# Induced attention and a leaky feed-forward net in one kernel: a first batch with later weights, unread products, maxima by column tiles, and half of the weight conversion on GpSimd

## The chip, the cores and the metric

The kernel runs on one core of a Trainium2 chip (trn2). The metric is the device time of one execution in microseconds; several executions give a median. The profile is one further execution, read by the hardware profiler. Engines are called as the profile calls them: PE is TensorE, PEld its weight loads, DVE is VectorE, ACT is ScalarE, POOL is GpSimd, SP is SyncE, which here issues nearly all transfers.

## The reference, cut to what matters

```python
def mab(q, kv):
    s = scale * (q @ kv.transpose(0, 2, 1))
    s = s - s.max(-1, keepdims=True)
    a = np.exp(s)
    a /= a.sum(-1, keepdims=True) + 1e-09
    return a @ kv
h = mab(I, x)                     # x: 4 batches of 12480 rows of 128; I: 32 inducing rows
x = mab(x, h).reshape(49920, 128)
h = x @ w_in                      # 128 -> 2048
g = np.maximum(0.01 * h, h)
return (g @ w_out).astype(np.float32)
```

The weights `w_in` and `w_out` reach the chip as 64-bit floats: pairs of 32-bit words that the kernel must turn into 32-bit floats itself.

## The kernel before, in words

**Tiling.** A batch of 12480 rows is six groups of 2048 rows (g0 to g5, each four tiles of 512 tokens) and a rest of 192 rows (`RG`). There are 98 tiles in all; after the first two ("quick") tiles, every tile runs through 16 blocks f of the hidden width. A tile's first products (`ffn_first`, 32 rows of the array each, four in parallel) give a PSUM bank, ACT takes the rectified high part (`high`, L1140), DVE the low part (`low`, L1144), and `ffn_second` or `products` multiplies both by `w_hi` and `w_lo` (three products). A rectified block can also be finished on POOL instead of DVE: ACT writes `g`, POOL makes a cast (`ghi`, L1114 or L1445) and a subtraction (`glo`, L1116 or L1447). This is called a far pair below.

**The first batch** (`first_batch`, L692) is written out by hand. SP issues 25 loads of x (`xr`, four per group) with a load of a weight chunk (`raw`, 512 KB) after the loads whose index is in `LOADS`. Then seven rounds follow, one per group in the order RG, g0, ..., g5. A round transposes its group on PE (`turn`, L725, 16 transposes) and copies it with ACT (L731), spreads the running maximum of the group before (`spread`, L478, called in `running`), multiplies the weighted rows of the group two before (L578) and computes its own scores (`columns_product`, L398). After the last round `DRAIN` lists what goes between the last steps, up to `normalise`, which gives h. In `ROUNDS` and `DRAIN` a string of letters stands for each place in that order: l steps the weight conversion, t and d turn a chunk of `w_in`, k issues an unread product.

**Weight conversion** (`from_double`, L198). Eight chunks (four of `w_in`, four of `w_out`), each of 128x512 values: a scaled copy on ACT (L211), then on DVE a mask (L216), a shift and or (L220), another mask (L226) and a product (L230), then one sum on POOL (L235). For `w_out` a chunk is then split: ACT casts `w_hi` (L286) and POOL subtracts to get `w_lo` (L288). These two are emitted by `parts_of_w_out` once the chunk's conversion has been emitted.

**The two quick tiles.** `quick` (L1023) computes the second attention of tiles 0 and 1 in a short way; its exponential `qy` (L1044) is an ACT instruction that the first `ffn_first` depends on through `A`. The two tiles are then multiplied alternately, four blocks at a time (`rounds`), with full-array second products (L1202). Blocks f = 4c to 4c+3 need chunk c of `w_hi` and `w_lo`. Between the blocks `others(u)` steps the rest of the conversion (`late`) and other lanes; u counts the blocks of both tiles.

**The rest** (`turn_over`, from tile 2 on) is ordered by a planner that runs while the kernel is built: it keeps a clock per engine, chooses the next instruction by the earliest start, and gathers those PE instructions that use the array in another tiling into clusters, since each switch of tiling costs time. `PATIENCE`, `IDLE`, `HURRY`, `AHEAD`, `PACE` are its waiting times in ns, and `WAITS` (38 numbers in us) delays the clusters one by one.

Engines execute their own instructions in the order in which they stand: an instruction that waits holds all behind it on that engine.

## Time and profile before

| what | us |
|---|---|
| median of 3 runs | 1435.7 |
| lowest and highest | 1434.36, 1436.16 |
| the profiled execution | 1436.48 |
| span of its instructions | 1434.7 |

| engine | busy us | share of the span |
|---|---|---|
| PE | 1418.0 | 99% |
| PEld | 1301.2 | 91% |
| POOL | 1178.9 | 82% |
| DVE | 1070.6 | 75% |
| ACT | 1066.0 | 74% |

A busy share counts an instruction from its start to its end, and PE's products overlap, so 99% does not say that no time is lost there. The chain of work that ended last, followed back from the last instruction, is PE for 94% of the span. A line such as L1171 can be a helper that many callers use.

### The profile page before, as it was taken

How to read it: one execution, taken by the hardware profiler on the slowest of the kernel's cores; microseconds unless marked ns; L12 is line 12 of the kernel's file. 1: busy time of each engine (PE TensorE's matmuls, PEld its weight loads, DVE VectorE, ACT ScalarE, POOL GpSimd, SP SyncE). 2: the span in 40 equal slices, each digit the busy share in tenths (PEclk: the TensorE clock that was granted, in tenths of full speed). 3: DMA queues.
4: the chain of work that ended last, by engine and by line, in shares of the span. 5: the costliest groups of instructions: out<-in, count | busy, mean ns of one | idle time of the engine just before them, and what ended most of it. 6: DMA issues, size and time to landing. Idle time of an engine off the chain costs nothing.

```text
span 1434.7 us, 60214 instructions
## 1 busy us (share of the span) xinstructions
PE 1418.0 (99%) x25207; PEld 1301.2 (91%) x25207; DVE 1070.6 (75%) x1913; ACT 1066.0 (74%) x1956; POOL 1178.9 (82%) x1237
## 2 busy tenths in 40 slices
PE   8999999999999999999999999999999999999998
PEld 6679899998889899998899999999989999999997
DVE  6777787776777787877777777877787876777664
ACT  6567777777777777777777787777777877778775
POOL 2369999899999888899999998885557588969996
PEclk9999999999999999999999999999999999999999
DMA  8055556433454553464445445534222333233231
GB/s 297 13 115 101 107 109 123 97 82 86 97 99 89 116 94 56 75 146 107 99 91 95 88 84 111 114 87 110 57 61 59 64 63 66 45 64 69 56 67 23
DMA packets 400703, 128.49 MB, mean 90 GB/s; under 512 B 373136, under 2 KB 375600, under 8 KB 400432
## 3 DMA queue, kind: packets, MB, share of 16 engines
q1 hardware_dynamic: 399328, 124.50, 41.7%
q8 instruction: 198, 3.24, 1.0%
q14 instruction: 73, 0.60, 0.1%
q10 hardware_dynamic: 1104, 0.15, 0.1%
HBM read 48.94 MB, written 25.56 MB: 52 GB/s over the span
## 4 chain that ended last, share of the span: by engine, by line
PE 94%; DVE 2%; ACT 1%; DMA 1%; issue 1%; POOL 1%; SPq 1%; DVEq 0%; ACTq 0%; POOLq 0%
PE bank L1171 87%; PE bank L398 3%; PE bank L578 2%; PE bank L1202 1%; DVE glo L1144 1%; PE bank L725 1%; DMA xr<-in_x_dram 1%; ACT ghi L1140 0%; DMA out_dram<-osb 0%; PE bank L820 0%; SPq L1012 0%; ACT xT L731 0%; POOL glo L1447 0%; PE bank L1058 0%; SPq L703 0%
## 5 line engine op out<-in xcount | busy, mean ns | idle before, releaser
L1171 PE MATMUL bank<-glo,w_hi 32*128 32x512 f32 (+1 forms) x6080 | 1165.1, 375 | 0.0
L1171 PE MATMUL bank<-ghi,w_hi 32*128 32x512 f32 (+1 forms) x6080 | 1164.7, 375 | 0.2
L1171 PE MATMUL bank<-ghi,w_lo 32*128 32x512 f32 (+1 forms) x6080 | 1164.8, 374 | 0.0
L1171 PE MATMUL bank<-A,hwhi 32*128 32x512 f32 (+1 forms) x3394 | 993.6, 373 | 0.8 <-DVE glo L1144 0.4
L1144 DVE SCALAR_TENSOR_TENSOR glo<-bank,ghi 128x512 fp32r<-128x512 f32 (+1 forms) x1047 | 687.2, 681 | 254.1 <-ACT ghi L1140 241.4
L1171 PEld LDWEIGHTS bank<-ghi,w_hi 32*128 32x128 f32 x6080 | 805.1, 184 | 16.5 <-issue 2.7
L1171 PEld LDWEIGHTS bank<-ghi,w_lo 32*128 32x128 f32 x6080 | 807.0, 184 | 12.4 <-issue 2.0
L1171 PEld LDWEIGHTS bank<-glo,w_hi 32*128 32x128 f32 x6080 | 806.8, 184 | 11.8 <-issue 1.0
L1140 ACT ACTIVATE ghi<-bank 128x512 fp32r<-128x512 f32 (+1 forms) x1047 | 608.0, 597 | 151.3 <-PE bank L1171 128.4
L1447 POOL TENSOR_TENSOR glo<-g,ghi 128x512 fp32r<-128x512 f32 (+1 forms) x513 | 656.0, 1279 | 41.1
L1171 PE MATMUL bank<-A,hwlo 32*128 32x512 f32 (+1 forms) x1697 | 586.2, 370 | 0.0
L1171 PEld LDWEIGHTS bank<-A,hwhi 32*128 32x128 f32 x3394 | 564.9, 184 | 16.6 <-DVE glo L1144 2.4
L1140 ACT ACTIVATE g<-bank 128x512 f32<-128x512 f32 (+1 forms) x521 | 311.2, 598 | 146.7 <-PE bank L1171 87.5
L1445 POOL CAST ghi<-g 128x512 fp32r<-128x512 f32 (+1 forms) x513 | 312.9, 610 | 106.5 <-ACT g L1140 80.0
L1171 PEld LDWEIGHTS bank<-A,hwlo 32*128 32x128 f32 x1697 | 299.9, 184 | 2.6 <-issue 0.2
L1481 DVE TENSOR_TENSOR part<-bank,part 128x512 f32<-128x512 f32 (+1 forms) x190 | 130.0, 685 | 60.7 <-PE bank L1171 38.3
L1492 POOL TENSOR_TENSOR part<-part 128x512 f32<-128x512 f32 (+1 forms) x95 | 121.4, 1277 | 22.5 <-DVE part L1481 22.1
L1474 ACT COPY part<-bank 128x512 f32<-128x512 f32 (+1 forms) x190 | 110.7, 584 | 12.4 <-PE bank L1171 10.5
L1229 DVE STREAM_TRANSPOSE osb<-part 128x512 f32<-128x512 f32 (+1 forms) x95 | 66.6, 701 | 6.6 <-POOL part L1492 4.9
L534 DVE STREAM_TRANSPOSE xT<-xc 128x512 f32<-128x512 f32 x72 | 46.5, 684 | 0.0
L455 ACT ACTIVATE e<-e,nm 128x512 f32<-128x512 f32 (+1 forms) x28 | 18.7, 667 | 22.9 <-DVE least L443 22.7
L936 POOL TENSOR_TENSOR y<-y,mx 128x512 f32<-128x512 f32 (+1 forms) x24 | 24.4, 1018 | 9.6 <-DVE mx L932 8.3
(135 smaller groups left out, 646.1 us busy)
## 6 DMA issues: line engine op xcount, KB each, us to landing
A<-both SPq DMA_DIRECT2D x376, 128.0 KB, 2.4
xr<-in_x_dram SPq DMA_DIRECT2D x96, 256.0 KB, 4.3
out_dram<-osb SPq DMA_DIRECT2D x382, 64.0 KB, 2.2
xc<-in_x_dram SPq DMA_DIRECT2D x288, 64.0 KB, 2.9
raw<-in_moe_w_in_dram SPq DMA_DIRECT2D x4, 512.0 KB, 6.6
raw<-in_moe_w_out_dram SPq DMA_DIRECT2D x4, 512.0 KB, 7.4
A<-both SPq DMA_DIRECT2D x48, 16.0 KB, 1.8
out_dram<-osb SPq DMA_DIRECT2D x48, 8.0 KB, 1.8
```

Source lines behind the costliest of these rows:

```text
L398: nc.tensor.matmul(dst, lhsT, rhs, start=True, stop=True)
L534: nc.vector.transpose(t[:, j, :], blk.rearrange("p n c -> p (n c)"))
L578: nc.tensor.matmul(hp[32 * k : 32 * k + 32, :C], ay[:rows_, 4 * q + k, :], xb[:rows_, k, :], start=(q == 0), stop=(4 * q + 4 >= K), tile_p ...
L1140: nc.scalar.activation(ghi, ph, AF.Relu)
L1144: nc.vector.scalar_tensor_tensor(out=glo, in0=ph, scalar=0.0, in1=ghi, op0=ALU.max, op1=ALU.subtract,)
L1171: nc.tensor.matmul(dst, w[32 * r : 32 * r + 32], woven(x[32 * r : 32 * r + 32]), start=start, stop=stop, tile_position=(32 * r, 0),)
L1229: nc.vector.transpose(osb[:, :n], total[:, :n])
L1445: nc.gpsimd.tensor_copy(ghi[:, :n], g[:, :n])
L1447: nc.gpsimd.tensor_tensor(out=glo[:, :n], in0=g[:, :n], in1=ghi[:, :n].bitcast(F32), op=ALU.subtract)
L1474: nc.scalar.copy(put, got)
L1481: nc.vector.tensor_tensor(out=put, in0=got, in1=put, op=ALU.add)
L1492: nc.gpsimd.tensor_tensor(out=total[:, :n], in0=total[:, :n], in1=part[:, :n], op=ALU.add)
```

## The change

1. `LOADS` moves every weight chunk's load four x loads (one group) later; the first chunk of `w_out` comes after the last x load.
2. `fill` issues products of the identity with itself that nobody reads: four in `setup`, and one at each f in `ROUNDS` and `DRAIN`.
3. `spread` always uses four column tiles with `e32`; before, the first batch used one full-array product.
4. `from_double`: the product that was one DVE instruction is two on POOL, so POOL now does a scaling of the low words (`tensor_scalar`), a product and the sum.
5. The steps of the conversion stand at other places: none in round g1 and before, steps in three rounds instead of four, other places in `DRAIN`, two more in the list after it, and in `others` one at every u below 8.
6. The planner's numbers change; `WAITS` has 37 entries.

```diff
-    LOADS = [4, 8, 12, 16, 20]
+    LOADS = [8, 12, 16, 20, 24]
...
     ROUNDS = [
-        ["", ""],
-        ["", "", "", "", "", "ll", ""],
-        *[["l", "l", "", "", "lll", "", "", ""]] * 4,
+        ["f", ""],
+        ["", "", "", "", "", "ff", ""],
+        [""] * 8,
+        *[["l", "l", "", "", "lll", "", "", ""]] * 3,
         ["l", "l", "", "", "l", "", "tt", ""],
     ]
-    DRAIN = ["", "", "ll", "lldkk", "", ""]
+    DRAIN = ["ll", "", "l", "lldkk", "llf", "f"]
...
-    EARLY, PREFER, YIELDING, PATIENCE = 250.0, 0.0, 200.0, 6000.0
-    IDLE, HURRY, APART, TAIL, WAITING, SOON = 1300.0, 1000.0, 60000.0, 5000.0, 3500.0, 3000.0
+    EARLY, PREFER, YIELDING, PATIENCE = 250.0, 0.0, 200.0, 8000.0
+    IDLE, HURRY, APART, TAIL, WAITING, SOON = 1100.0, 5500.0, 60000.0, 5000.0, 3500.0, 3000.0
...
     WAITS = [
-        12.8, 12.2, 0.1, 3.6, 1.0, 0.0, 6.6, 0.7, 0.0, 4.7, 0.0, 0.8, 8.8, 0.0,
-        1.1, 4.2, 7.6, 6.1, 10.9, 0.0, 4.0, 0.0, 3.2, 0.0, 9.8, 0.0, 5.7, 6.3,
-        8.3, 0.0, 9.5, 6.4, 7.7, 8.6, 2.7, 0.2, 9.2, 6.4,
+        12.8, 12.2, 0.1, 3.6, 0.0, 1.5, 6.6, 0.0, 0.8, 4.2, 0.0, 0.8, 2.5, 0.0,
+        1.1, 1.7, 7.6, 6.1, 10.9, 0.0, 4.0, 0.0, 3.2, 0.0, 9.8, 0.0, 5.7, 6.3,
+        12.1, 0.0, 9.1, 6.4, 7.7, 8.6, 2.8, 0.0, 4.7,
     ]
-    AHEAD = 100.0
-    PACE, STOCK = 41250.0, 4
+    AHEAD = 150.0
+    PACE, STOCK = 36000.0, 4
...
-        nc.vector.scalar_tensor_tensor(
-            out=tail, in0=low.bitcast(U32), scalar=2.0**-52, in1=b.bitcast(F32),
-            op0=ALU.mult, op1=ALU.mult,
-        )
-        spent(POOL, 1270.0, spent(DVE, 690.0))
+        nc.gpsimd.tensor_scalar(
+            out=tail, in0=low.bitcast(U32), scalar1=2.0**-52, scalar2=None, op0=ALU.mult
+        )
+        nc.gpsimd.tensor_tensor(out=tail, in0=tail, in1=b.bitcast(F32), op=ALU.mult)
         nc.gpsimd.tensor_tensor(out=dst, in0=a.bitcast(F32), in1=tail, op=ALU.add)
+        spent(POOL, 3400.0, clock[DVE])
...
+    FILLERS = 4
+
+    def fill():
+        while True:
+            pt = gen_ps("fill_ps")
+            nc.tensor.matmul(pt[:, :P], ident, ident, start=True, stop=True)
+            done(pt)
+            yield
...
+        for _ in range(FILLERS):
+            next(filling)
         pt = aux_ps("ind_ps")
...
-        if not quads[0]:
-            same = e128.rearrange("p j m -> p (j m)")
-            nc.tensor.matmul(dst, same, src, start=True, stop=True)
-            return on_array("f", 64.0, at, taken[0])
         for k in range(4):
...
-            one, weights, two, one, weights, one, weights, one, keep, one, two, late, one, two,
+            one, late, weights, two, one, weights, one, weights, one, late, keep, one, two, late, one, two,
...
-            if u % 2 == 0:
+            if u % 2 == 0 or u < 8:
                 step(late)
```

What the letters do to the order of the instructions is seen at three places. In the changed kernel's rows the lines are 10 to 14 higher (L300 is what L286 was, L1054 what L1044 was).

DVE at the end of the first batch, before (L597 adds up h, L324 copies a turned chunk, L1036 begins the quick tile):

```order
L597 SCALAR_TENSOR_TENSOR hacc<-hacc,al,bank_69 128x128
L656 TENSOR_SCALAR rz<-bank_71 128x1
L657 RECIPROCAL rz<-rz 128x1
L216 TENSOR_SCALAR cv_b<-raw 128x512
L597 SCALAR_TENSOR_TENSOR hacc<-hacc,al,bank_64 128x128
L220 SCALAR_TENSOR_TENSOR cv_a<-cv_a,cv_b 128x512
L226 TENSOR_SCALAR cv_b<-cv_a 128x512
L324 COPY winT<-bank_65 128x512
L1036 TENSOR_REDUCE qmx<-bank_71 128x4
```

The same place after the change:

```order
L607 SCALAR_TENSOR_TENSOR hacc<-hacc,al,bank_69 128x128
L666 TENSOR_SCALAR rz<-bank_71 128x1
L667 RECIPROCAL rz<-rz 128x1
L607 SCALAR_TENSOR_TENSOR hacc<-hacc,al,bank_65 128x128
L217 TENSOR_SCALAR cv_b<-raw 128x512
L221 SCALAR_TENSOR_TENSOR cv_a<-cv_a,cv_b 128x512
L338 COPY winT<-bank_66 128x512
L227 TENSOR_SCALAR cv_b<-cv_a 128x512
L1046 TENSOR_REDUCE qmx<-bank_71 128x4
```

Before, the chunk converted here is the second of `w_out` (the sixth of all); after, it is the first of `w_out` (the fifth), with its second mask behind the copy of the turned chunk.

ACT at the same time, before (`hs` and `hT` end the first batch, L1044 is the quick tile's exponential):

```order
L211 ACTIVATE cv_a<-raw 128x512
L674 ACTIVATE hs<-hacc,rz 128x128
L684 COPY hT<-bank_70 128x128
L286 CAST w_hi<-wraw 128x512
L1044 ACTIVATE qy<-qy 128x128
L805 ACTIVATE hwhi<-bank_70 128x512
L1064 CAST A_685<-bank_67 128x512
```

And after:

```order
L212 ACTIVATE cv_a<-raw 128x512
L684 ACTIVATE hs<-hacc,rz 128x128
L694 COPY hT<-bank_70 128x128
L300 CAST w_hi<-wraw 128x512
L212 ACTIVATE cv_a<-raw 128x512
L1054 ACTIVATE qy<-qy 128x128
L815 ACTIVATE hwhi<-bank_70 128x512
L1074 CAST A_721<-bank_67 128x512
```

The cast of the first chunk of `w_hi` stands ahead of the exponential in both; a further chunk's scaled copy has come between them.

POOL from the first `w_lo` on, before:

```order
L288 TENSOR_TENSOR w_lo<-wraw,w_hi 128x512
L235 TENSOR_TENSOR wraw<-cv_a,cv_t 128x512
L288 TENSOR_TENSOR w_lo<-wraw,w_hi 128x512
L1114 CAST ghi<-g 128x512
L1116 TENSOR_TENSOR glo<-g,ghi 128x512
L1114 CAST ghi<-g 128x512
L1116 TENSOR_TENSOR glo<-g,ghi 128x512
```

And after:

```order
L302 TENSOR_TENSOR w_lo<-wraw,w_hi 128x512
L1124 CAST ghi<-g 128x512
L1126 TENSOR_TENSOR glo<-g,ghi 128x512
L1124 CAST ghi<-g 128x512
L1126 TENSOR_TENSOR glo<-g,ghi 128x512
L231 TENSOR_SCALAR cv_t<-raw 128x512
L234 TENSOR_TENSOR cv_t<-cv_t,cv_b 128x512
L235 TENSOR_TENSOR wraw<-cv_a,cv_t 128x512
L302 TENSOR_TENSOR w_lo<-wraw,w_hi 128x512
```

The second chunk of `w_out` stood ahead of the first two far pairs and now stands behind them.

## Rows read from the trace of the kernel before

**Rows 1.** Stretches: length, busy time and count by engine, granted clock, DMA share, GB/s.

```profile
91.34:1417.00 1325.66, 1324.20 (x24391) 1234.29 (x24390) 997.21 (x1731) 1008.09 (x1838) 1140.53 (x1198) 1.00 0.43 87
...
11.86:15.27 3.41, 3.41 (x18) 3.41 (x18) 0.53 (x2) 1.75 (x3) 0.00 (x0) 0.50 1.02 396
15.27:31.30 16.03, 15.84 (x206) 11.46 (x205) 15.42 (x52) 14.30 (x32) 5.63 (x4) 1.00 1.04 367
```

**Rows 2.** Chain that ended last, first 50 us in order: start, length, what.

```profile
11.74 3.62 PE bank L725 x16
...
25.28 1.90 PE bank L725 x16
...
29.36 0.60 PE bank L725 x4
...
39.87 0.23 PE bank L680 x2
...
42.21 0.32 ACT qy L1044
...
45.42 0.70 PE bank L1171 x8
```

**Rows 3.** The last x load of the first batch: its issue and its time to landing.

```profile
L703 SPq DMA_DIRECT2D xr<-in_x_dram x1: 328/328/328, 23.5 to 23.5; - x1
...
DMA to landing us min/median/max: 6.4/6.4/6.4
```

**Rows 4.** DVE in order of time, end of the first batch: start, length, instruction.

```profile
38.49 0.35 DVE L597 SCALAR_TENSOR_TENSOR hacc<-hacc,al,bank 128x128 f32<-128x128 f32 x1 [0.34 <-PE bank L578]
38.75 0.69 DVE L220 SCALAR_TENSOR_TENSOR cv_a<-cv_a,cv_b 128x512 int32<-128x512 int32 x1
...
39.81 0.68 DVE L324 COPY winT<-bank 128x512 f32<-128x512 f32 x1
```

**Rows 5.** ACT in order of time, the same place.

```profile
36.84 0.68 ACT L211 ACTIVATE cv_a<-raw 128x512 f32<-128x512 f32 x1
...
40.29 0.62 ACT L286 CAST w_hi<-wraw 128x512 fp32r<-128x512 f32 x1
```

**Rows 6.** POOL in order of time, quick tiles.

```profile
50.78 1.27 POOL L288 TENSOR_TENSOR w_lo<-wraw,w_hi 128x512 fp32r<-128x512 f32 x1 [4.08 <-ACT w_hi L286]
...
56.47 0.61 POOL L1114 CAST ghi<-g 128x512 fp32r<-128x512 f32 x1 [1.45 <-ACT g L1140]
57.16 1.29 POOL L1116 TENSOR_TENSOR glo<-g,ghi 128x512 fp32r<-128x512 f32 x1
```

**Rows 7.** PE in order of time, quick tiles.

```profile
60.24 0.48 PE L1202 MATMUL bank<-ghi,w_hi 128*128 128x512 f32 x1
...
71.74 0.48 PE L1202 MATMUL bank<-ghi,w_lo 128*128 128x512 f32 x1 [0.32 <-POOL w_lo L288]
...
74.31 1.64 PE L1171 MATMUL bank<-A,hwhi 32*128 32x512 f32 x4
...
82.65 0.48 PE L1202 MATMUL bank<-ghi,w_lo 128*128 128x512 f32 x1 [0.64 <-POOL w_lo L288]
```

**Rows 8.** Stretches of row-tiled products alone (L1171): length, PE and PEld busy.

```profile
277.48:317.27 39.79, 39.79 (x731) 37.72 (x731) 1.00 0.34 78
...
592.66:636.66 44.00, 43.59 (x792) 41.74 (x792) 1.00 0.46 94
...
1282.56:1417.02 134.46, 134.40 (x2446) 130.45 (x2446) 1.00 0.29 58
```

**Rows 9.** DVE masks, and a small scaling: durations in ns, min/median/max.

```profile
L216 DVE TENSOR_SCALAR cv_b<-raw x8: 381/428/1294, 9.8 to 69.2; 128x512 int32<-128x512 int32 x8
...
L953 DVE TENSOR_SCALAR sm<-sm x28: 124/547/1054, 65.1 to 1315.1; 128x16 f32<-128x16 f32 x24, 96x2 f32<-96x2 f32 x4
```

**Rows 10.** DVE and POOL in order of time, 68.9 to 70.6 us.

```profile
68.93 1.27 POOL L1116 TENSOR_TENSOR glo<-g,ghi 128x512 fp32r<-128x512 f32 x1
...
69.25 1.29 DVE L216 TENSOR_SCALAR cv_b<-raw 128x512 int32<-128x512 int32 x1
```

3 lines of the change are left out of this document (2 added, 1 removed).

## The prediction

> **What bounds the kernel now.** I read the stretches first, then the chain of waits in order of time, then each engine's instructions in order around the places that the change touches. From 91.3 us to 1417 us PE is busy for 1324.2 of 1325.7 us [rows 1]: the change can touch this part only through the pace of the products. The first 91 us are another matter. The chain there runs from a transfer to 11.74 us, when PE begins the transposes of the second full group; from then on it is PE, round after round, one round being 29.36 - 25.28 = 4.08 us [rows 2]. After the last transposes it is a chain of short dependent steps, through the quick tile's exponential at 42.21 us to the first feed-forward product at 45.42 us [rows 2]. In the two quick tiles PE is nearly closed up, but here and there it waits for a chunk of `w_lo` from POOL [rows 7]. So the question is what the change does to the chain of the first 91 us.
>
> My sum is made against the profiled execution, 1436.48 us, which is 0.8 us above the median of 1435.7; at the end I take the 0.8 off. A difference of 0.2%, 2.9 us here, is about what a measurement of this kernel can tell from none.
>
> **The change part by part.**
>
> *Later weights, unread products, column tiles (the first batch).* They work on one stretch, so they go together. What they can bring has a floor. The last x load was issued at 23.5 us and landed 6.4 us later, at 29.9 us [rows 3]. The transfers were full from 15 to 31 us, at 367 GB/s [rows 1]. One weight chunk of 0.52 MB now comes behind the last x load, which is worth 0.52 / 367 GB/s = 1.4 us: the load lands at 28.5. A quarter of its group's 16 transposes takes 1.90 / 4 = 0.5 us [rows 2], so the transposes cannot end before 29.0; before they ended at 29.36 + 1.90 = 31.26. **The gain is 2.3 us at most.** That the second group's transposes took 3.62 us at a granted clock of 0.50 (1.2 GHz) [rows 1, 2] instead of 1.90 at 2.4 GHz is part of the same 2.3 us and not to be added. The cheaper spread saves part of its time in each round, inside the same floor. The other end is nothing, if the rounds stay 4.08 us long for another reason (see the lock below). I take -1.2, the middle.
>
> *The unread products near the end.* One stands ahead of the product that makes hT, which is on the chain. The nearest row, a product of the same size, took 0.23 us [rows 2]: +0.2, between 0 and 0.3. The ones at the start lie in time in which PE has no data.
>
> *The cast of `w_hi` ahead of the exponential.* This is a new wait, and the largest doubt about the change. ACT has, in this order, the first cast of `w_hi`, now also a scaled copy of 0.68 us [rows 5], and then the exponential. Before, the chunk to be cast had been ready for long: the cast ran at 40.29 with no wait in front of it [rows 5]. Now this chunk is a conversion later, and its last DVE mask stands behind a mask, a shift-or and the copy of a turned chunk. I count from the last sum of h, which ended at 38.49 + 0.35 = 38.84 [rows 4]. Then DVE does a mask (0.43, the median in [rows 9]), a shift-or (0.69), the copy of a turned chunk (0.68) [rows 4] and a mask (0.43): 41.07. POOL does a product and a sum, for which its two-input row stands, 1.29 each [rows 6]: 43.65. Its scaling of the low words needs only the raw load and runs ahead. ACT casts (0.62) and copies (0.68) [rows 5]: the exponential can start at 44.95 instead of 42.21. All later work hangs on it: **+2.7**. If successive DVE instructions overlap a little, as the starts at 38.75 and 39.81 allow, it is 2.3; with one blocked instruction more it is 4.0.
>
> *PE's clock in that wait.* PE has only odd products while it waits. Before, a wait for x at the start was followed by 3.4 us at 1.2 GHz [rows 1]. If that comes again it can cost half of 3.4, 1.7 us; else nothing. Since part of that stretch is waiting anyway, I take +0.4.
>
> *The second chunk of `w_out`.* Behind two far pairs on POOL it becomes late. The second pair ended at 57.16 + 1.29 = 58.45 [rows 6]. Then POOL does the scaling: no row shows it; a cast of the same shape took 0.61 and a two-input operation 1.29 [rows 6], and as it reads one tensor I take 0.7. Product and sum make 2.58: 61.73. The cast on ACT, 0.62: 62.35. PE wants this chunk of `w_hi` at 60.24 [rows 7], so it stands for 2.1 us. POOL's subtraction takes 1.27 [rows 6]: `w_lo` is there at 63.62, while PE could use it 0.3 us after `w_hi`: another 1.0 us. **+3.1**; 2.7 with every price at its low end, 4.4 with one instruction blocked. Meanwhile ACT holds the next rectified blocks back behind the cast, but PE is late by more than they are.
>
> *What this repays.* PE waited 0.32 and 0.64 us for the third and fourth chunks of `w_lo`, and four first products at 74.31 took 1.64 us, where the usual four take about 0.5 [rows 7]. With PE 3 us later, and the third chunk no longer behind a far pair, most of it goes: -1.5, between 0 and -2.1.
>
> *Less conversion on DVE, the planner's numbers.* In the rest, the order shows 46 low parts fewer on DVE and 46 far pairs more on POOL, and one entry less in `WAITS`. A pair is 0.61 + 1.29 = 1.9 us [rows 6], 87 us in all; POOL had 1326 - 1141 = 185 us free [rows 1]. What PE gains depends on the pace. A clean stretch runs at 39.79 / 731 = 54.4 ns a product, two slow ones at 55.6 and 55.0 [rows 8]; at the clean pace these two would give 0.9 and 1.3 us. I set the low end at twice their sum, -4.5, since other stretches are slow too, and the high end at +2, for new waits for POOL. No row says which, so I take 0.
>
> **The sum:** -1.2 + 0.2 + 2.7 + 0.4 + 3.1 - 1.5 + 0 = +3.7 us, 1440.2 for an execution like the profiled one, 1439.4 for the median.
>
> **The lock.** A DVE mask began at 69.25 while POOL's subtraction ran until 70.20, and took 1.29 us instead of 0.43; eight such masks go up to 1294 ns, and a small scaling from SBUF to SBUF, 28 times, has a median of 547 and goes from 124 to 1054 [rows 9, 10]. So some DVE instructions wait until POOL's instruction is over. The change makes POOL busy for 0.7 + 2.58 = 3.3 us per chunk in rounds of 4.08 us, while DVE still does two masks and a shift-or for the next chunk. The Trainium skill (SBUF — State Buffer, Who interferes with whom) says that DVE and GpSimd share a port pair as an exclusive lock: a DVE instruction in a two-port mode, or with two SBUF inputs against a GpSimd instruction that reads SBUF, blocks for the other's whole instruction. By that rule the 1.29 us of this trace is the full wait and would meet all three conversion steps, the case of the first rival, 1444.2, against 1439.4 without it; the trace agrees for the masks.
>
> **The rivals.**
>
> *Blocked conversions (slower still).* The mechanism is the row at 69.25. In each of three rounds DVE would wait out the rest of a POOL instruction and another, 0.65 + 0.65 us, of which about half fits into DVE's spare time of a round: the gain of the first batch turns into about +1, and the two waits go to 4.0 and 4.4. The sum is then 1 + 0.2 + 4.0 + 0.4 + 4.4 - 1.5 = +8.5, 1444.2. For it speaks that the spread of durations is real; against it that half of the places lie where DVE waits for PE anyway.
>
> *The floor is reached and the waits are short (no change).* The first batch gives its 2.3, the clock stays up, both new waits cost their low ends and the old ones go: -2.3 + 0.2 + 2.3 + 2.7 - 2.1 = +0.8, 1436.5. For it: PE set the pace of the rounds, and its waits go with the new order of the loads.
>
> *The pace of the long part (not slower).* Moving 46 low parts off DVE closes the slow stretches. It decides from a mean of about 54.4 ns a product in the stretches that now take 55 and more. With the full 4.5 us the sum is -0.8, 1434.9; together with the case before it is -3.7, 1432.0, and faster. Against it: in [rows 8] PE is busy throughout, and POOL would be at 93%.
>
> *The unread products do not hold the clock.* Then the second group's transposes again run at 1.2 GHz and the first batch gives nothing: +4.9, 1440.6.
>
> **How the numbers follow.** The forecast has 0.45, with a range of its own from 1437.5 to 1442; blocked conversions 0.09, the floor 0.23, the pace of the long part 0.17, the clock 0.06. The predicted time is the forecast's, 1439.4. Slower by over 0.2% means above 1438.6: four fifths of the forecast, the blocked conversions and the clock, 0.51. Within 0.2%: the rest of the forecast, most of the floor and part of the pace, 0.36. Faster: the pace with the floor, 0.13. The range from 1432.5 to 1442.5 leaves out the blocked conversions and the best of the combined case.
>
> **What would show it.** Right: the first feed-forward product comes later than 45.4 us, with ACT idle in front of the cast of `w_hi` until a POOL sum; PE waits some 2 us for the second chunk's `w_hi`, released by ACT, and then for `w_lo`; the row-tiled part begins near 95 us instead of 91.3; DVE masks of over 0.6 us among the conversions. Wrong: no such idle time on ACT, a first product before 44 us, or a long part shorter than 1322 us.

## The result, and the profile after

The changed kernel takes 1452.85 us (median of 6 runs, 1448.51 to 1454.95) against 1435.74 us (6 runs, 1434.09 to 1436.16): a ratio of 1.0115, 95% interval 1.0105 to 1.0126. The forecast was 1439.4 with a range up to 1442.5. The sign was right; of some 17 us it had 3.7. The six executions of the changed kernel do not agree well: two lie at 1448.5 to 1448.7 us and four at 1452.8 to 1455.0.

The profiled execution took 1448.73 us with a span of 1446.9. Three places cut the time of either profile into four stretches: the last score products of the first batch (the line L398, after the change L412), the first second-product of the quick tiles (L1202, L1212), and the first row-tiled product behind the last of those. They can be read off each profile's PE in order of time; the last stretch ends with PE's last product.

| stretch, us | before | after | difference |
|---|---|---|---|
| start to the last score products | 32.09 | 31.18 | -0.91 |
| from there to the first second-product | 15.23 | 18.31 | +3.08 |
| from there to the row-tiled part (quick tiles) | 44.02 | 55.38 | +11.36 |
| row-tiled part | 1338.42 | 1337.14 | -1.28 |
| sum | 1429.76 | 1442.01 | +12.25 |

So 12.25 us of the 17 can be found in these two profiles, and nearly all of them lie in the quick tiles. The profiled execution is one of the two short ones; the other 4 to 5 us of the median lie outside it (see "Two executions of one kernel"). Stretches of the changed kernel, in the columns of [rows 1]:

```profile
65.84:71.30 5.46, 4.89 (x15) 3.94 (x16) 4.71 (x7) 3.72 (x8) 5.18 (x4) 0.50 0.10 14
71.30:83.66 12.36, 12.36 (x86) 8.28 (x85) 11.99 (x22) 5.76 (x11) 6.28 (x7) 1.00 0.28 44
83.66:87.82 4.16, 0.16 (x1) 0.00 (x0) 0.13 (x1) 0.02 (x1) 3.95 (x3) 1.00 0.18 28
87.82:95.40 7.58, 6.50 (x23) 4.67 (x27) 3.59 (x7) 2.84 (x6) 2.28 (x2) 0.55 0.67 124
104.87:1429.27 1324.40, 1324.23 (x24392) 1234.24 (x24391) 971.01 (x1684) 1003.74 (x1838) 1222.45 (x1292) 1.00 0.43 87
```

From 83.66 to 87.82 every engine but POOL stands still. Behind the two long waits PE works at a mean granted clock of 0.50 and 0.55 (the lower of its two levels, 1.2 GHz, for all or most of the stretch). The last line is what [rows 1] had as 1325.66 us.

PE of the changed kernel in order of time, the waits that are new against [rows 2, 7]:

```profile
31.18 1.07 PE L412 MATMUL bank<-xT,indT 128*32 128x512 f32 x8 [1.14 <-ACT xT L741]
...
40.02 0.49 PE L246 MATMUL bank<-ident 128*128 128x128 f32 x2 [1.39 <-DVE winT L338]
40.34 0.39 PE L690 MATMUL bank<-e,hs 128*128 128x128 f32 x2
...
49.49 0.48 PE L1212 MATMUL bank<-ghi,w_hi 128*128 128x512 f32 x1 [0.68 <-ACT ghi L1150]
...
65.84 0.79 PE L1212 MATMUL bank<-ghi,w_hi 128*128 128x512 f32 x1 [3.35 <-ACT w_hi L300]
67.20 0.79 PE L1212 MATMUL bank<-ghi,w_lo 128*128 128x512 f32 x1 [0.56 <-POOL w_lo L302]
...
87.82 1.50 PE L363 MATMUL bank<-wraw,winT 128*128 128x128 f32 x8 [4.00 <-POOL wraw L235]
...
91.69 0.80 PE L839 MATMUL bank<-w,hT 128*128 128x128 f32 x2 [1.08 <-DVE w L369]
```

POOL at the two long waits, where [rows 6] showed the far pairs with the conversion already done:

```profile
55.23 0.61 POOL L1124 CAST ghi<-g 128x512 fp32r<-128x512 f32 x1 [10.18 <-ACT g L1150]
...
59.33 1.29 POOL L1126 TENSOR_TENSOR glo<-g,ghi 128x512 fp32r<-128x512 f32 x1
60.71 1.75 POOL L231 TENSOR_SCALAR cv_t<-raw 128x512 f32<-128x512 uint32 x1
62.54 1.26 POOL L234 TENSOR_TENSOR cv_t<-cv_t,cv_b 128x512 f32<-128x512 f32 x1
63.88 1.26 POOL L235 TENSOR_TENSOR wraw<-cv_a,cv_t 128x512 f32<-128x512 f32 x1
...
79.93 1.05 POOL L946 TENSOR_TENSOR y<-y,mx 128x512 f32<-128x512 f32 x1 [2.35 <-DVE mx L942]
81.50 0.61 POOL L1124 CAST ghi<-g 128x512 fp32r<-128x512 f32 x1 [0.52 <-PE bank L1212]
82.19 1.27 POOL L1126 TENSOR_TENSOR glo<-g,ghi 128x512 fp32r<-128x512 f32 x1
83.55 1.53 POOL L231 TENSOR_SCALAR cv_t<-raw 128x512 f32<-128x512 uint32 x1
85.17 1.26 POOL L234 TENSOR_TENSOR cv_t<-cv_t,cv_b 128x512 f32<-128x512 f32 x1
86.51 1.26 POOL L235 TENSOR_TENSOR wraw<-cv_a,cv_t 128x512 f32<-128x512 f32 x1
```

Both times the conversion starts when the far pair ahead of it ends, and takes more than 4 us. Ahead of the first far pair POOL had stood idle for 10.18 us, waiting for `g`, with the conversion behind it. What the conversion's product needs from DVE, the second mask (56.90 us, 0.59 long), was there at 57.49; the product began at 62.54. ACT, in front of the exponential and of the casts:

```profile
43.09 0.62 ACT L300 CAST w_hi<-wraw 128x512 fp32r<-128x512 f32 x1 [2.06 <-POOL wraw L235]
...
44.17 0.30 ACT L1054 ACTIVATE qy<-qy 128x128 f32<-128x128 f32 x1
...
65.17 0.62 ACT L300 CAST w_hi<-wraw 128x512 fp32r<-128x512 f32 x1 [5.12 <-POOL wraw L235]
```

In [rows 5] the first cast had no wait in front of it.

### The profile page after: what moved, and what is told of

Same layout as the page of the kernel before. It is cut to its first block, busy times and chain, and to the rows that moved or that the text cites. A ratio compares the mean times of both kernels' runs of the same rounds, so it can differ in the third digit from the quotient of the medians.

```text
span 1446.9 us, 60529 instructions
## 1 busy us (share of the span) xinstructions
PE 1424.1 (98%) x25273; PEld 1304.3 (90%) x25273; DVE 1044.6 (72%) x1859; ACT 1060.4 (73%) x1956; POOL 1281.7 (89%) x1345
## 4 chain that ended last, share of the span: by engine, by line
PE 62%; ACT 0%; DVE 0%; issue 0%; DVEq 0%; ACTq 0%
PE bank L1181 59%; PE bank L412 1%; PE bank L1212 1%; PE bank L588 1%; PE bank L830 0%; DVE glo L1154 0%; ACT ghi L1150 0%; ACT g L1150 0%; PE bank L495 0%; PE bank L690 0%; DVE osb L1243 0%; PE bank L842 0%; DVEq L1771 0%; PE bank L1224 0%; ACTq L1150 0%
## 5 line engine op out<-in xcount | busy, mean ns | idle before, releaser
L1181 PE MATMUL bank<-A,hwhi 32*128 32x512 f32 (+1 forms) x3394 | 982.6, 374 | 0.2 <-DVE A L1077 0.2
L1154 DVE SCALAR_TENSOR_TENSOR glo<-bank,ghi 128x512 fp32r<-128x512 f32 x1001 | 659.4, 682 | 288.7 <-ACT ghi L1150 272.8
L1181 PEld LDWEIGHTS bank<-glo,w_hi 32*128 32x128 f32 x6080 | 797.8, 184 | 13.5 <-issue 2.8
L1457 POOL TENSOR_TENSOR glo<-g,ghi 128x512 fp32r<-128x512 f32 x560 | 716.0, 1279 | 44.9
L1150 ACT ACTIVATE ghi<-bank 128x512 fp32r<-128x512 f32 x1001 | 580.7, 597 | 143.1 <-PE bank L1181 125.6
L1150 ACT ACTIVATE g<-bank 128x512 f32<-128x512 f32 (+1 forms) x567 | 338.8, 598 | 161.6 <-PE bank L1181 101.3
L1455 POOL CAST ghi<-g 128x512 fp32r<-128x512 f32 x560 | 341.4, 610 | 43.7 <-ACT g L1150 39.5
L1006 POOL TENSOR_TENSOR both<-aT,both 128x512 fp32r<-128x512 f32 x24 | 31.2, 1298 | 2.3 <-ACT both L999 2.3
```

What stands on the lines that cost most here:

```text
L1006: (eng or nc.gpsimd).tensor_tensor(out=alo[sl], in0=aT.pop((b, g))[: 32 * J, :], in1=ahi[sl].bitcast(F32), op=ALU.subtract,)
L1150: nc.scalar.activation(ghi, ph, AF.Relu)
L1154: nc.vector.scalar_tensor_tensor(out=glo, in0=ph, scalar=0.0, in1=ghi, op0=ALU.max, op1=ALU.subtract,)
L1181: nc.tensor.matmul(dst, w[32 * r : 32 * r + 32], woven(x[32 * r : 32 * r + 32]), start=start, stop=stop, tile_position=(32 * r, 0),)
L1455: nc.gpsimd.tensor_copy(ghi[:, :n], g[:, :n])
L1457: nc.gpsimd.tensor_tensor(out=glo[:, :n], in0=g[:, :n], in1=ghi[:, :n].bitcast(F32), op=ALU.subtract)
```

## The experiments

Each run is read by the same stretches, of its profiled execution, whose own time is in the column ahead of the median; the ratio is that of several runs to those of the kernel before.

| run | to the last scores | to the first second-product | quick tiles | row-tiled | profiled | median | ratio, 95% interval |
|---|---|---|---|---|---|---|---|
| before | 32.09 | 15.23 | 44.02 | 1338.42 | 1436.48 | 1435.7 | |
| after | 31.18 | 18.31 | 55.38 | 1337.14 | 1448.73 | 1452.85 | 1.0115 (1.0105 to 1.0126) |
| e1 | 30.82 | 17.78 | 50.32 | 1342.54 | 1448.46 | 1447.68 | 1.0082 (1.0065 to 1.0099) |
| e2 | 31.47 | 15.22 | 47.55 | 1346.89 | 1447.89 | 1447.0 | 1.0078 (1.0063 to 1.0093) |
| e3 | 30.77 | 19.57 | 48.99 | 1340.96 | 1447.01 | 1447.44 | 1.0081 (1.0066 to 1.0096) |
| e4 | 30.86 | 19.29 | 65.11 | 1337.14 | 1459.12 | 1458.65 | 1.0159 (1.0144 to 1.0175) |
| e5 | 33.20 | 17.78 | 50.64 | 1338.57 | 1447.66 | 1446.43 | 1.0073 (1.0058 to 1.0088) |
| e6 | 32.41 | 15.22 | 45.09 | 1338.15 | 1437.59 | 1436.85 | 1.0006 (0.9996 to 1.0015) |
| e7 | 34.87 | 19.26 | 53.16 | 1337.14 | 1451.16 | 1451.33 | 1.0115 (1.0100 to 1.0130) |
| e8 | 31.84 | 15.92 | 44.06 | 1339.38 | 1437.93 | 1436.58 | 1.0008 (0.9998 to 1.0018) |
| e9 | 30.75 | 20.31 | 45.90 | 1336.66 | 1440.33 | 1438.43 | 1.0024 (1.0015 to 1.0033) |
| e10 | 31.23 | 17.78 | 49.41 | 1337.90 | 1443.26 | 1441.21 | 1.0037 (1.0024 to 1.0050) |
| e11 | 32.79 | 19.29 | 55.61 | 1337.24 | 1451.65 | one run | |
| e12 | 33.52 | 19.17 | 55.74 | 1337.27 | 1452.44 | 1451.33 | 1.0112 (1.0099 to 1.0126) |
| e13 | 30.87 | 17.91 | 55.35 | 1337.18 | 1448.04 | 1450.02 | 1.0108 (1.0093 to 1.0124) |
| e14 | 32.83 | 17.89 | 45.59 | 1336.34 | 1439.37 | 1439.6 | 1.0027 (1.0017 to 1.0038) |
| e15 | 32.02 | 15.22 | 45.08 | 1339.50 | 1438.56 | one run | |
| e16 | 31.66 | 15.22 | 44.04 | 1341.77 | 1439.40 | 1439.45 | 1.0020 (1.0010 to 1.0030) |

### The product alone, and the planner's order

**e1** is the changed kernel with the product back on DVE (the edit shown); **e2** is the kernel before with the product on POOL, the same edit the other way round:

```diff
-        nc.gpsimd.tensor_scalar(
-            out=tail, in0=low.bitcast(U32), scalar1=2.0**-52, scalar2=None, op0=ALU.mult
-        )
-        nc.gpsimd.tensor_tensor(out=tail, in0=tail, in1=b.bitcast(F32), op=ALU.mult)
+        nc.vector.scalar_tensor_tensor(
+            out=tail, in0=low.bitcast(U32), scalar=2.0**-52, in1=b.bitcast(F32),
+            op0=ALU.mult, op1=ALU.mult,
+        )
+        spent(POOL, 1270.0, spent(DVE, 690.0))
...
-        spent(POOL, 3400.0, clock[DVE])
```

> The changed kernel with only the conversion's product back in one DVE instruction, so that POOL does the sum alone. Theory A, the three steps on POOL: a chunk costs POOL 1.28 us instead of the 4.3 us that the changed kernel shows (1.75 + 1.26 + 1.26), the two long waits of PE (3.35 us for the second chunk of w_hi, 4.00 us for the fourth chunk) shrink to under 1 us each, and the two stretches at a granted clock of 0.50 behind them go. The row-tiled part then begins at 90 to 93 us instead of 104.9, and the median is 1434 to 1439. Rival B, the new places: the steps stand later and behind the far pairs wherever the product runs, so a wait of over 2 us stays; the part begins after 98 us, 1443 to 1449. Rival C, the planner's numbers and the long part: the median stays above 1449.

> The kernel before with only the product moved to the two POOL instructions; loads, rounds, places and planner's numbers as before. Theory A: POOL spends about 3 us more on each of eight chunks; the last three chunks of w_out come late and PE waits 2 us or more at least once in the quick tiles, with the clock at 0.50 behind it; 1440 to 1448. Rival B: in the old places the POOL steps lie in time that POOL has free (it was idle for most of the first 50 us), so no wait of PE over 1 us; 1435 to 1438. Rival D, the blocked DVE instructions: masks and shifts of over 0.9 us in the rounds, the last transposes end after 32.3 us (31.26 before), and the loss lies before 46 us.

Both lose 11 us. By the time alone e1 would fit its rival B and e2 its theory A, but for a good part of the loss no theory had the place. The quick tiles lose 6.3 us in e1 and 3.5 in e2, but 4.1 and 8.5 us lie in the row-tiled part: the `spent` of the edit moves the planner's clocks, and so the order of the whole rest, while `WAITS` stays. So the two runs say little of the product; **e5** and **e6** repeat them with the `spent` line left as it was. PE and ACT then have the order of the kernel each comes from, instruction for instruction.

> The changed kernel with the product in one DVE instruction, and the planner's clocks left as if it were on POOL, so that every other instruction keeps its place on every engine. The run with the same edit and the planner's clocks changed too began the row-tiled part at 98.9 us (104.9 in the changed kernel) and then took 1342.5 us for it (1337.1). Theory: the 5.4 us in the row-tiled part came from the changed order alone, so here it is 1337.1 within 0.5; and the product on POOL costs 6 us of the front in these places, so the part begins at 97 to 99.5 us: profile 1437.5 to 1441. Rival, the row-tiled part is slower because DVE or POOL enter it later or earlier: it stays above 1340 and the time above 1443. Rival, the places cost nothing once the product is off POOL: the part begins before 93.5 us, 1436 or less.

> The kernel before with the product in two POOL instructions, and the planner's clocks left as before, so that every other instruction keeps its place. With the clocks changed too, the part began at 94.2 us (91.3 before) and took 1346.9 us (1338.4). Theory: the row-tiled part is 1338.4 within 0.5 here, and the POOL product in the old places costs the front 2 to 4 us: the fourth chunk of w_out late by 2 to 3 us, the granted clock at 0.50 behind it; profile 1438.5 to 1441. Rival, the product on POOL by itself is what slows the row-tiled part: it stays above 1343 and the time above 1445.

The row-tiled part comes back, to 1338.57 and 1338.15 (1.4 over and 0.3 under the kernel each comes from), so the order had made the difference in e1 and e2. What is left is a square of four for the quick tiles: old places with DVE 44.02, with POOL 45.09; new places with DVE 50.64, with POOL 55.38. ("New places" stands for all the rest of the change; the unread products and column tiles alone, e8, give 44.06, and the planner's numbers alone, e16, 44.04.) Profiles that repeat a corner agree with it within 0.4 us: 45.08 in e15, 55.35 to 55.74 in e11 to e13. The product on POOL costs 1.1 us in the old places, where 2 to 4 were expected, and the new places cost 6.6 without it; together they cost 11.4. e5 missed its ranges for the time, by the part of the loss that stays and by a late start (33.20). The two longest of PE's four waits for chunks in e6:

```profile
79.88 1.16 PE L349 MATMUL bank<-wraw,winT 128*128 128x128 f32 x8 [1.11 <-POOL wraw L234]
...
84.03 0.48 PE L1202 MATMUL bank<-ghi,w_lo 128*128 128x512 f32 x1 [0.86 <-POOL w_lo L288]
```

With the same product on POOL none is over 1.2 us (the other two are 0.59 and 0.84), and the clock stays up.

**e16** takes the planner's numbers alone.

> The kernel before with only the planner's numbers of the change; loads, first batch and conversion as before. The row-tiled part took 1337.1 us in the changed kernel, 1338.4 before, and up to 1346.9 where an edit changed the planner's clocks and so its order while the 37 or 38 numbers of WAITS stayed. Theory: those numbers are fitted to one order of work; here they meet another one, and the row-tiled part is 1338 to 1347, the front as before (44.0 us for the quick tiles): 1436 to 1445. Rival, the numbers are better by themselves: 1337 or less and 1434.5 or less.

They make the row-tiled part 3.4 us longer, not shorter: 0.2% slower. So the 1.3 us that the row-tiled part gained in the changed kernel do not come from the numbers alone. They are about as large as what one order can differ by: e6 and e15, with the same order, have 1338.15 and 1339.50. Still, the six profiles with the changed kernel's order and product (after, e4, e7, e11, e12, e13) have 1337.14 to 1337.27, and the four with the order of the kernel before (before, e6, e8, e15) 1338.15 to 1339.50.

### The place

**e3** keeps far pairs off POOL until the last chunk of `w_out` has been emitted:

```diff
-        if far_ends[-2:-1] <= [start] and max(clock[POOL], start + RELU) + FAR_HIGH + FAR_LOW < (
+        if len(ready) == NF // 4 and far_ends[-2:-1] <= [start] and max(clock[POOL], start + RELU) + FAR_HIGH + FAR_LOW < (
```

> The changed kernel in which no far pair goes to POOL before the last chunk of w_out has been emitted; DVE makes those low parts. Three pairs (1.9 us each) leave POOL's order ahead of the second and fourth conversion. Theory A: both long waits need the length of the conversion and the pairs ahead of it; the first shrinks from 3.35 to under 1.5 us, the second from 4.0 to under 2 us, at least one stretch at 0.50 goes; median 1440 to 1446 against 1452.9. If the length alone makes the wait, the waits stay above 2.5 us and the median above 1449. If DVE with three more low parts of 0.6 us becomes late, the masks are what the conversion waits for, and the gain is under 3 us.

The first long wait is gone, the second falls to 1.37 us, and the quick tiles gain 6.4 us; 3.8 us are lost again in the row-tiled part, whose order is another, and the median misses its range of 1440 to 1446 by that. **e9** moves the conversion itself. It is two steps further on when the first products begin, with its masks on DVE and scaled copies on ACT, and every other instruction stays where it was (the planner's clocks are kept by a lane that only counts; those lines of the edit are not shown):

```diff
...
+        for _ in range(2):
+            step(late)
...
         first_round(*rounds[0])
```

> The changed kernel with its conversion two steps further on when the first feed-forward products begin: the second mask and the three POOL instructions of the second chunk of w_out now stand ahead of the first far pairs, and every later chunk is two steps earlier. POOL keeps the product, the loads and the first batch keep the change, all other instructions keep their order. Theory: the loss comes from the place, the conversion reaching POOL behind work of the quick tiles; the waits of 3.35 + 0.56 us and of 4.00 us go to under 0.5 us each, and the stretches at 0.50 behind them with them. From the last score products to the row-tiled part it takes 61 to 65 us instead of 73.7 (59.3 in the kernel before); the row-tiled part stays at 1337.1 to 1338.6; profile 1437 to 1441, median 1438 to 1442. Rival, the length of the three POOL instructions is enough by itself: waits of 2 us or more stay at one of the two places, 68 us or more. Rival, the steps moved ahead hold the first products: the first second-product comes over 1 us later than the 18.3 us behind the last score products that it takes in the changed kernel.

Two steps take back 14 us of the median's 17: 1438.43. Between the two profiles it is 8.4 us, and the quick tiles alone gain 9.5. The three POOL instructions stay on POOL, so the place alone makes this difference. POOL, where the chunk that PE waited for now stands ahead of the far pairs, and the only wait of PE over 0.6 us in the quick tiles:

```profile
44.72 1.51 POOL L227 TENSOR_SCALAR cv_t<-raw 128x512 f32<-128x512 uint32 x1
50.45 1.27 POOL L230 TENSOR_TENSOR cv_t<-cv_t,cv_b 128x512 f32<-128x512 f32 x1 [4.22 <-DMA xc<-in_x_dram]
51.80 1.27 POOL L231 TENSOR_TENSOR wraw<-cv_a,cv_t 128x512 f32<-128x512 f32 x1
58.27 0.61 POOL L1134 CAST ghi<-g 128x512 fp32r<-128x512 f32 x1 [5.21 <-ACT g L1160]
```

(The bracket at 50.45 names a transfer; the second mask on DVE ended there too, 49.88 + 0.42.)

```profile
85.49 0.49 PE L849 MATMUL bank<-w,hT 128*128 128x128 f32 x2 [1.01 <-DVE w L379]
```

The rival that the steps hold the first products is met in its number: the first second-product is 2.0 us later than in the changed kernel. But in this execution the clock was low just there, and e14 below, with the same two steps, has 17.89 instead of 20.31:

```profile
41.00:54.50 13.50, 12.82 (x104) 7.83 (x104) 8.33 (x21) 4.80 (x10) 6.88 (x6) 0.51 0.05 7
```

**e10** puts the product back on DVE as well.

> The same two steps ahead, and the product in one DVE instruction. Theory: both causes are gone, so the stretch from the last score products to the row-tiled part is that of the kernel before or a little more, 59 to 62 us; with the later weights the last score products come 0.9 us earlier in an execution whose x loads land early, and up to 3 us later in one where they land late; the row-tiled part is 1337.1 to 1338.6 against 1338.4. Profile 1433 to 1437, median 1433.5 to 1437, no worse than the kernel before. Rival, something else in the first 105 us was spoilt (the unread products, the column tiles): over 64 us for the stretch and over 1439.

The theory falls here: it had 1433.5 to 1437, and the median is 1441.21. The quick tiles take 49.41 us, against 45.90 in e9 and 45.59 in e14, which have the product on POOL. So with the conversion ahead POOL is the better place for the product in these profiles; the medians of e9 and e10 differ by 2.8 us, and their intervals overlap a little. Of the 3.5 us, the profile shows 0.82 us at the third second-product and 1.98 in place of 1.01 at the product of `w` and hT (both released by DVE), and a granted clock of 0.68 from 84 to 88 us; why DVE is late there was not separated.

### The clock

**e4** and **e7** put unread products ahead of the two long waits: e4 with a PSUM bank from the usual ring, e7 with one that is free.

```diff
+                if (t, f) == (0, TURN):
+                    unread(banks[next(i for i in turns["aux"] if i not in held)], 15)
                 at = ffn_second(t, f)
```

> The changed kernel with unread products put into its two long waits: 15 of the identity ahead of the first product that needs the second chunk of w_hi, 18 ahead of the transposed products of the fourth chunk. They leave the waits as they are. Theory: the granted clock of 0.50 from 64 to 71 us and from 89 to 95 us comes from the idle time of PE before it; with PE kept busy both stretches go, which is worth about (0.63 - 0.38) / 0.63 of some 11 us of products, 4 to 5 us: profile near 1444, median 1444 to 1449. Rival: the clock falls for another reason, or the products are too few: no change, 1448 to 1455.

> The changed kernel with 15 and 18 unread products ahead of the two long waits once more, now into PSUM banks that are free at that time (in the first try they had themselves to wait for a bank, until DVE had made a low part, 6.63 and 5.88 us). Nothing else moves. Theory: the waits stay (PE's last instruction ahead of them ends when it did, the first real product begins as before, at about 65.8 and 87.8 less what was gained), the two stretches of 0.50 go, the part begins at 99 to 101.5 us instead of 104.9; profile 1443 to 1446, median 4 to 5 us under the changed kernel's 1452.9. Rival, the clock does not follow PE's idle time: no change, 1448 to 1455. Rival, it follows only in part: 2 us.

The edit shown is the first of the two places in e7. e4 is 6 us slower: the unread products wait for their own bank, 6.63 and 5.88 us, released by a low part on DVE. In e7 they run through both waits, and no stretch of 0.50 follows:

```profile
67.05 3.62 PE L254 MATMUL bank<-ident 128*128 128x128 f32 x30
70.49 0.48 PE L1218 MATMUL bank<-ghi,w_hi 128*128 128x512 f32 x1
71.84 0.48 PE L1218 MATMUL bank<-ghi,w_lo 128*128 128x512 f32 x1 [0.87 <-POOL w_lo L306]
...
95.82 0.49 PE L845 MATMUL bank<-w,hT 128*128 128x128 f32 x2 [2.05 <-DVE w L375]
```

So at these two places the clock follows PE's idle time. Holding it is worth 55.38 - 53.16 = 2.2 us in the quick tiles, half of what was expected: the next waits grow, 0.56 to 0.87 and 1.08 to 2.05. The median, 1451.33 against 1452.85, does not show it clearly: this profile had the latest start of all (34.87).

### The first products

**e8** gives the kernel before the unread products and the column tiles; **e12** takes the last two unread products out of the changed kernel; **e13** moves its first cast of `w_hi` behind the exponential; **e14** is e9 with the edits of e12 and e13.

```diff
-    DRAIN = ["ll", "", "l", "lldkk", "llf", "f"]
+    DRAIN = ["ll", "", "l", "lldkk", "ll", ""]
...
-        step(splits)
...
-            one, late, weights, two, one, weights, one, weights, one, late, keep, one, two, late, one, two,
+            one, weights, two, one, splits, late, weights, one, weights, one, late, keep, one, two, late, one, two,
```

> The kernel before with the unread products of the change (four in the setup, one at each f) and the maxima by column tiles; the loads, the conversion and the planner's numbers as before. If the unread products hold the clock, the transposes that took 3.6 us at 0.50 near 12 us take 1.9 us. Theory: the pace of the rounds is then set by the transfers, which end at about 30 us, so the last transposes end at 30.5 to 31.3 instead of 31.26; the unread products near the end cost 0.2; 1434.5 to 1436.5, no difference that can be measured. Rival, PE sets the pace: 1.0 to 1.7 us go, 1434.5 or less.

> The changed kernel without the last two unread products of the first batch, those around the product that makes hT. In the changed kernel the first of them waits 1.39 us for a PSUM bank that a DVE copy has not yet left, and the product behind it, whose input was there at 38.0, starts at 40.34. Theory: hT comes 1.5 to 2.3 us earlier, but the exponential stays behind the cast of w_hi, which waits for POOL until 43.1, so the first second-product still comes 18.3 us behind the last score products and the time does not move: 1448 to 1454. Rival, the unread product was on the chain: 1.5 to 2.3 us earlier, 1446.5 to 1452. Rival, the wait at that bank is where PE's clock falls in some executions: without it no stretch at 0.50 near 41 to 50 us, and the executions lie closer together, near 1449.

> The changed kernel with the first cast of w_hi and the scaled copy behind it moved behind the exponential on ACT; nothing else moves. My prediction gave 2.7 us to this wait. Theory: the exponential starts when DVE has subtracted the maximum, at 42.8 instead of 44.2, since the unread product still holds the chain ahead of it: 1.3 us of the 18.3 us from the last score products to the first second-product go, 16.8 to 17.2 us remain; profile about 1447, median 1.3 under 1452.9. Rival, all 2.7 us were the cast: 15.6 us. Rival, the cast was covered: 18.3 us.

> The two edits together (no late unread products, the cast behind the exponential) on the kernel with the conversion two steps ahead, which took 1438.4. Theory: with both holds gone the first second-product comes 15 to 16 us behind the last score products (18.3 in the changed kernel, 15.2 in the kernel before), the clock does not fall near 41 us, and from there to the row-tiled part it takes 44.0 to 45.9 us; the row-tiled part 1336.7 to 1337.2. Profile 1433.5 to 1436.5, median 1433.5 to 1436.5: level with the kernel before or up to 2 us under it. Rival, the two steps ahead of the first products cost 1.5 us by themselves and the clock falls: 1437 to 1439.

e8: no difference that can be measured (1436.58 against 1436.0). The unread product near the end waits 0.68 us for a bank there, which is the 0.7 us to the first second-product. e12: without it hT comes earlier (the product behind it at 40.81 - 33.52 = 7.3 us after the last scores instead of 9.2), but the exponential does not, since the cast still waits for POOL:

```profile
41.23 0.27 ACT L694 COPY hT<-bank 128x128 f32<-128x128 f32 x1 [0.86 <-PE bank L690]
45.43 0.62 ACT L300 CAST w_hi<-wraw 128x512 fp32r<-128x512 f32 x1 [3.94 <-POOL wraw L235]
```

The rival on the clock falls too: the clock is low without that bank as well (a mean of 0.60 from 48 to 52 us). e13 gains 0.4 us, not 1.3. Its exponential does start 1.3 us earlier, 42.54 - 30.87 = 11.67 us behind the last scores instead of 12.99, but the multiplication of `qy` on DVE that follows it took 0.29 us in the changed kernel and takes 1.28 here, beside POOL's subtraction:

```profile
43.62 1.28 DVE L1060 TENSOR_TENSOR qy<-qy,qsm 128x128 f32<-128x128 f32 x1
```

```profile
43.49 1.27 POOL L302 TENSOR_TENSOR w_lo<-wraw,w_hi 128x512 fp32r<-128x512 f32 x1 [0.73 <-ACT w_hi L300]
```

e14's first second-product comes at 17.89, no better than e13's, though its exponential runs 9.79 us behind the last scores, earlier than in the kernel before (10.12); and its median, 1439.6, is no better than e9's:

```profile
42.62 0.31 ACT L1064 ACTIVATE qy<-qy 128x128 f32<-128x128 f32 x1 [1.82 <-DVE qy L1060]
44.74 0.62 ACT L311 CAST w_hi<-wraw 128x512 fp32r<-128x512 f32 x1 [1.81 <-POOL wraw L231]
...
45.86 0.58 ACT L825 ACTIVATE hwhi<-bank 128x512 fp32r<-128x512 f32 x1
46.34 0.58 ACT L1084 CAST A<-bank 128x512 fp32r<-128x512 f32 x1
```

Here the wait for POOL has moved behind the exponential: the same cast now stands ahead of `hwhi` and `A`, which the first products need too, and the multiplication on DVE takes 1.15 us, beside POOL's sum. So their order on ACT is worth little as long as the chunk comes this late from POOL; the parts of what e14 loses behind its exponential were not separated.

### Two executions of one kernel

> The changed kernel once more, for a second profile: its executions lie in two groups, 1448.5 to 1448.7 and 1452.8 to 1455. Theory: the first x loads land at times that differ by 2 us, PE's clock comes up 2 to 5 us later when it has to wait there, and since the rounds are paced by PE at 4.36 us nothing takes this up; and the clock falls at about 41 us in some executions. If this profile is of the upper group, the last score products stand at 33 to 35 us instead of 31.2, or a stretch at 0.50 between 41 and 50 us is seen, or both; the row-tiled part has the same length, 1337.1, in either group.

It took 1451.65 us, between the two groups, and shows both effects: the last score products at 32.79, and a clock of 0.50 from 44 to 48 us. The start, in the changed kernel's first profile and then in e11:

```profile
9.93 1.07 PE L412 MATMUL bank<-xT,indT 128*32 128x512 f32 x8
10.93 1.97 PE L735 MATMUL bank<-ident,xr 128*128 128x128 f32 x16
```

```profile
7.97 1.11 PE L735 MATMUL bank<-ident,xr 128*128 128x128 f32 x4 [0.21 <-DMA xr<-in_x_dram]
...
10.39 1.94 PE L412 MATMUL bank<-xT,indT 128*32 128x512 f32 x8
```

The same score products take 1.07 us in one and 1.94 in the other. In the first profile PE is at full speed from 9.9 us, in e11 some 2 us later. Of all profiles with the changed first batch, in five (e5, e7, e11, e12, e14) the four transposes behind the fifth x load take 1.11 to 1.12 us, after a wait of 0.21 to 1.57 us for that load, and the last score products come at 32.79 to 34.87; in three (e1, e4, e10), which waited 0.31 to 0.42 us, they take 0.66 us, and the last score products come at 30.82 to 31.23; the other four did not wait, 30.75 to 31.18. So a wait for x at the low clock goes with a late start; a wait at full speed does not, and neither do slow transposes without a wait (1.06 us in the changed kernel's first profile and in e13). What brings the clock up earlier in one execution than in another was not separated. The unread products do not settle it: e5 and e7 have them and are slow up to the second group (1.10 and 1.12 us for its first four transposes), and e2, e6 and e16, the kernel before without them, are at full speed there (0.66 us).

With the change nothing takes a late start up, because a round now takes 27.80 - 23.43 = 4.37 us. Part of this is a wait: 0.33 us ahead of the score products of most rounds, for ACT's copy of the transposed x. On ACT the conversion's scaled copy has moved between the first of these copies and the other three, with ACT idle ahead of them (e8, with the column tiles and the old places, has its last round in 29.00 - 25.00 = 4.0 us). After the change and before it, in the last round:

```profile
28.50 0.59 ACT L741 COPY xT<-bank 128x512 f32<-128x512 f32 x1 [0.85 <-PE bank L735]
28.98 0.70 ACT L212 ACTIVATE cv_a<-raw 128x512 f32<-128x512 f32 x1
29.57 1.55 ACT L741 COPY xT<-bank 128x512 f32<-128x512 f32 x3
```

```profile
29.26 0.68 ACT L211 ACTIVATE cv_a<-raw 128x512 f32<-128x512 f32 x1
29.99 2.05 ACT L731 COPY xT<-bank 128x512 f32<-128x512 f32 x4
```

The transposes of the third full group begin 2.3 us earlier than before (14.72, 17.02), the last score products only 0.9: 1.4 us are lost in between. The kernel before, with rounds of 4.08 us and in some profiles a wait for x in mid-batch, has its last score products at 31.47 to 32.41 in all its variants.

e11 is 2.9 us longer than the first profile, 1.6 of it in the start and 1.0 up to the first second-product. No execution of the upper group has a profile, so it is only likely that the rest of the median's loss lies in the same two stretches.

### The price of the scaling

**e15** is e6 with the scaling reading the high words as floats.

```diff
-            out=tail, in0=low.bitcast(U32), scalar1=2.0**-52, scalar2=None, op0=ALU.mult
+            out=tail, in0=high.bitcast(F32), scalar1=2.0**-52, scalar2=None, op0=ALU.mult
```

> The kernel before with the product on POOL and every instruction in its old place, in which POOL's scaling reads the high words as 32-bit floats instead of the low words as unsigned integers; the step between the words read, 8 bytes, is the same. (The low part of every converted weight is wrong by that.) The scaling takes 1.5 to 1.9 us in all runs so far, where I had put 0.7. Theory: the integer input is what costs, and it takes 0.6 to 0.8 us here. Rival: the step of 8 bytes between the words costs, and it stays at 1.5 us or more. Rival: scaling is dearer on POOL than a cast whatever it reads, 1.0 to 1.3 us. The time is that of the kernel with the integer input, 1436.9, or up to 1 us less.

Durations of that line in e6 and in e15, min/median/max in ns:

```profile
L230 POOL TENSOR_SCALAR cv_t<-raw x8: 1521/1652/2008, 9.6 to 75.4; 128x512 f32<-128x512 uint32 x8
```

```profile
L230 POOL TENSOR_SCALAR cv_t<-raw x8: 1523/1614/1940, 9.3 to 75.0; 128x512 f32<-128x512 f32 x8
```

The integer input costs nothing that can be seen. The rival on the step of 8 bytes stands, but scaling from words that lie side by side was not tried, so the step is not shown to be the cause. The one time, 1438.56, is 1.7 us over the expected 1436.9; against e6's profile the row-tiled part is 1.35 us longer, with the same order.

## Why the prediction was right in sign and far off in size

**First batch, -1.2: near in the profile, for another sum, and not in general.** The last transposes end at 27.80 + 1.97 = 29.77 instead of 31.26, and the last score products come 0.9 us earlier. Behind this stand transposes of the third full group that begin 2.3 us earlier (no wait for x ahead of the second group, 1.41 us before, and full speed in it) and rounds that are 0.3 us longer, which I had as a little shorter or the same. That the two nearly gave my number is luck. And with the changed first batch the executions differ by 4 us in this place (30.75 to 34.87): at its worst the start is 2.8 us later than before, where I had "nothing" as the high end. I had no term for that; it is the likely place of most of the 4 to 5 us by which the median's loss is larger than the profile's.

**Unread products, +0.2: wrong price, no effect.** One waits 1.39 us for a bank; I had priced its run and not its bank. The cast covers it.

**Cast ahead of the exponential, +2.7: right size, cause half named.** The exponential starts 12.99 us behind the last score products instead of 10.12, +2.9, and the first second-product +3.1. By e13 the place of the cast holds the exponential for 1.3 us, of which 0.4 reach the first second-product; by e12 the unread product alone gives nothing, since the chunk is ready on POOL only later. **Clock in that wait, +0.4:** 0 in this profile; in e11 the stretch is another 1.0 us longer, with 0.50 from 44 to 48 us. The row on which I had built it shows no fall of the clock: the 16 transposes ahead of that wait for x had taken 3.76 us, as slow as those behind it.

**Second chunk, +3.1: right mechanism, one price too low.** PE waited 3.35 + 0.56 = 3.9 us. I had taken 0.7 us for the scaling, from the cast as its nearest row; it took 1.75. No row of the kernel before shows it, and the dearer of the two rows that I took it from, 1.29, is too low as well.

**Repayment, -1.5: right where it applies.** Counted from the first second-product, the 31st comes at 21.56 us in the changed kernel and the 61st at 33.41, in the kernel before at 15.14 and 29.00: 11.85 us instead of 13.86, -2.0.

**The step that failed** is the end of this chain. In the term for what the delay repays I wrote that with PE later and the third chunk no longer behind a far pair, "most of it goes", so I had no new wait for the fourth chunk, and did not ask what stands ahead of the fourth chunk. POOL's order had the answer: a subtraction, a far pair, then a conversion of 1.53 + 1.26 + 1.26 us that PE wanted when it began. Across that wait (4.00, and 1.08 behind it) the next six second-products take 42.64 - 33.41 = 9.2 us, slow ones among them, where the kernel before took 30.40 - 29.00 = 1.4: +7.8, by itself twice the forecast. (Some 1.2 us of this are only another order: the products of the fourth chunk with `winT` and of `w` with hT lie among these six here, and behind them before.) Second, I charged PE's clock to the wait of the first batch alone. The six second-products from the second chunk's first on take 5.21 us instead of 2.21, +3.0: 0.56 of it is the wait for `w_lo`, the rest slow products. With 3.4 up to that first product, 3.0 for these six, -2.0 repaid, 7.8 at the fourth chunk and -0.9 in what follows, the sum is +11.3, as measured.

**Planner and far pairs, 0 (-4.5 to +2): inside the range.** -1.3 in the changed kernel; the numbers alone, in the kernel before (e16), give +3.4.

**The rivals.** The blocked conversions were nearest in time and had the wrong mechanism: masks and shifts of up to 1.61 us are there (1.29 in [rows 10]), the median of the first mask rises from 0.43 to 0.76 us, and with the product on DVE again (e5) 6.6 us of the loss stay. Both long waits were released by POOL's own chain. The Trainium skill (SBUF — State Buffer, Who interferes with whom) gives an exclusive lock on the port pair that DVE and GpSimd share, and these durations agree with it; but that lock was not what the two long waits ended with. The floor and the pace are out. That the unread products do not hold the clock is out for the two long waits (e7), where the change has none; at the start, which that rival meant, the profiles leave it open.

**Beating both.** None of these kernels does. e6 and e8 are level with the kernel before, e9 is 0.24% behind it.

## What to carry to other kernels

When work moves to an engine that executes in order, go through every later place at which someone waits for that engine, to the last, and ask there what stands ahead and how long the moved piece takes; the first such place is not the dearest. Here a long wait of PE cost itself and then the slow products behind it. In a kernel whose order comes from a planner with fitted numbers, an experiment must hold the planner's clocks still, or it measures the planner.

## What the runs showed of the hardware that I had not expected

- A one-input scaling on POOL, from every second 32-bit word, takes 1.52 to 2.0 us for 128x512, more than a two-input product (1.27) and 2.6 times a cast (0.61); float words make no difference.
- After PE waits of 3.35 and 4.00 us the granted clock was 0.50 until 71 us and 95 us; with unread products in the waits it stayed at 1.00, which gave back 2.2 us.
- The row-tiled part, the same products in another order, took 1336.3 to 1346.9 us; in one order it came out up to 1.35 us apart.
- A multiplication of 128x128 on DVE, both inputs in SBUF, took 0.29 us, and 1.28 (e13) and 1.15 (e14) beside an instruction of POOL.
